# Attention and routed experts on one core: the second block's gathers in one run, and transposed probabilities in two tiles

## The chip, the core and the metric

The kernel runs on one core of one Trainium2 chip. The metric is the device time of one launch in microseconds, lower is better. Two executions of the same kernel differ by some tenths of a per cent.

## What is computed

Attention with rotary embedding over 8 batches, 8 heads, 576 tokens and 64 columns a head, then a mixture of 8 experts over the 4608 tokens, each token to the one expert with the highest logit:

```python
q_rot, k_rot = rotate(q), rotate(k)
scores = matmul(q_rot, k_rot.T) / sqrt(64)
attn = exp(scores - max(scores)); attn /= sum(attn) + 1e-9
x = matmul(attn, v)                      # as 4608 rows of 512
logits = x @ w_gate + modality_bias[modality_id]
e_idx = argmax(logits, axis=1); gate_w = softmax(logits)[e_idx]
for e in range(8):
    mask = e_idx == e
    h = maximum(x[mask] @ w1[e], 0.0)    # 512 -> 1024
    out[mask] = gate_w[mask, None] * (h @ w2[e])   # 1024 -> 512
```

Every matmul is in float32, most as three products of a high and a low part.

## The kernel before

**Attention.** The outer loop runs over 32 pairs of heads (`n`; four pairs are one batch). For each pair TensorE computes the scores in nine units (`scores`, tile `ps`), DVE takes the row minimum of the negated scores (`rowmin`, `mn`), ACT the exponential (`expo`, tile `P`). TensorE transposes the probabilities (`fill`), and ACT and DVE copy them out of PSUM (`evac`): into `PH` for the first 512 keys, 128 partitions x 8 x 576 queries, and into `PD` for the last 64 keys. `AV` multiplies them with V in two halves, queries 0 to 255 and 256 to 575. `outp`, `ev` and `xout` turn the result, scale it and write a batch of rows to the table `X` in device memory.

**Routing.** After each batch a chain of small steps (`route`) finds each token's expert and its place in the expert's list. `scatter` then writes token number and gate weight to the table `TAB`, in five indirect DMAs a batch, issued by GpSimd (POOL).

**Experts.** The tokens are worked in blocks of 256 (`s`). The first eight blocks are planned from the first five batches alone (`plan0`), so that they can begin before the routing of the last batches is done; a second plan covers the rest. A block's steps: `m_ix` loads its rows of `TAB` (tiles `ix`, `xi`); `m_gather` computes row numbers on POOL (`iy`) and issues eight indirect DMAs of 128 rows x 128 columns from `X` to `XG`, of which the first four are one half of the block and the last four the other; there are two `XG`, for even and odd blocks. `m_tr` transposes a half on DVE, `m_tre` copies it to the high part on ACT and subtracts on DVE for the low part (`HL<-XG`). `m_load1` and `m_load2` load weights to `ST1` and `ST2`, only where the expert changes; `m_hi` converts to the high part on ACT (`W1H`, `W2H`), `m_lo` subtracts on DVE (`W1L`, `W2L`). `m_l1` is the first layer (tile `psH`, 96 matmuls), `m_l1e` its relu, `m_l2` the second layer (`psY`, 48 matmuls), ACT's scaling by the gate (`sc`) and an indirect DMA of the output rows, on POOL.

**Order.** TensorE, ACT, DVE and POOL take their instructions in the order in which they are written, and this order comes from numbers: each step is a job with a key, a time within its pair of heads (`KEYS`, `EDGE`, `MOE`), and the jobs are sorted. A key above `end=25.0` in the last pair puts a job into the part behind the cut, where attention's PSUM is handed over and the steps follow in order of their keys; after them the block loop `chain` runs. SyncE's queue is written in this order up to the cut, and is ordered by the scheduler behind it. `AFTER` adds waits to single gathers, for instance for the latest first-layer matmul of block 0 that stands ahead (`'l1', 0`).

Of the kernel before, what the change touches and what calls it, by code (L numbers as in the profile page):

```python
# [8 lines left out]
F32 = mybir.dt.float32  # L9
# [9 lines left out]
P = 128  # L19
B, H, S, D = 8, 8, 576, 64  # L20
# [129 lines left out]
        "A_FB": 13.315, "B_FB": 14.059, "AVA": 14.280, "RE": 14.638, "A_F3": 14.844, "B_F3": 15.844, "OTA": 16.826, "AVB": 19.635,  # L150
# [3 lines left out]
    },  # L154
# [41 lines left out]
    setdma=(-353.070, -199.654, -64.082, -129.156),  # L196
    consts=(28.166, 28.282),
    plan=(-34.727, 16.183, -5.857, -25.884),
    ix=(-13.525, 17.418, 11.679, 11.775),
    w1=(-33.501, -27.735, 15.231, -22.655),  # L200
    w2=(-4.011, 1.762, 12.647, -8.483),
    hi=(-22.046, 1.027, 19.870, 16.903),
# [5 lines left out]
    l1=(17.301, 17.002, 22.720, 21.734),  # L208
    l1e=(22.809, 22.869, 24.662, 24.647),
    w1n=(20.502, 24.643, 23.254, 22.825),  # L210
    place=(10.490, 11.490),
    rows=(5.189, -7.595, 2.778, 1.170, -0.984, 8.071, 5.429, 11.766, 24.719, 23.818, 21.468, 24.323, 19.920, 20.117, 22.957, 17.444,
        18.250, 23.228, 17.169, 21.813, 22.941, 24.907, 21.508, 22.829),
    pl=(-114.356, -102.856, -99.906, -88.406, -85.506, -73.956, -51.417, -48.907, -45.303),
    end=25.0,
)
AFTER = {(0, 3): (30, 'av', 0), (0, 4): (30, 'av', 0), (0, 5): (30, 'av', 1), (0, 6): (30, 'av', 1), (0, 7): (30, 'out', 1), (1, 0): ('l1', 0), (1, 1): ('l1', 0), (1, 2): ('l1', 0), (1, 3): ('l1', 0), (1, 4): ('l1', 0), (1, 5): ('l1', 0), (1, 6): ('l1', 0), (1, 7): ('l1', 0)}
PIN = "PE,Activation,DVE,Pool"


# [1 line left out]
def tile_attention_moe(ctx: ExitStack, tc: tile.TileContext, qk, v, mod, wg, mb, w1, w2, rope, cf, ci, out):  # L222
# [43 lines left out]
    pp = ctx.enter_context(tc.tile_pool(name="pp", bufs=1))  # L266
# [7 lines left out]
    def place(i, name, **kw):  # L274
        return places[i].enter_context(tc.tile_pool(name=name, bufs=1, reuse_waits="tile", **(dict(side="right") if i == 0 else {}), **kw))
# [4 lines left out]
            [P, 8, DM], F32R, name="W2" + "HL"[i])  # L280

    P4 = pp.tile([P, S + 128], F32, name="P4")
    PD = pp.tile([P, S], F32, name="PD")
    Vs = [pp.tile([P, 2, 5, 64], F32, name=f"V{i}") for i in range(2)]


# [1 line left out]
    OT = [pp.tile([P, S], F32, name=f"oT{i}") for i in range(2)]  # L288
    pj = place(0, "pj")
    PJ = [pj.tile([P, 2 * S], F32, name=f"P{j}") for j in range(4)]  # L290
    PH = place(1, "ph").tile([P, 8, S], F32, name="PH")


    SL = [psS.tile([P, 2, 512], F32, name=f"ps{i}") for i in range(4)]
# [3 lines left out]
    def take(nm, bks):  # L298

        own = SLOTS[nm]  # L300
        if nm == "RK8":
            own, bks = own & 3, (own >> 2,)
        if not all((own, b) in idle for b in bks):
            if nm == "RK8":
                own, b = min(idle, key=idle.get)
                bks = (b,)
            else:
                own = min((i for i in range(4) if all((i, b) in idle for b in bks)), key=lambda i: max(idle[i, b] for b in bks))
        for b in bks:
            del idle[own, b]  # L310
        return (own, *bks) if nm == "RK8" else own

    def give(own, *bks):
        for b in bks:
            idle[own, b] = clock[0]
            clock[0] += 1
# [36 lines left out]
    def setup():  # L353
        g = nc.gpsimd
        v_ = nc.vector
        v_.memset(EPS, 1e-9)
        v_.memset(ZERO, 0.0)
        v_.memset(PD, 0.0)
        v_.memset(P4, 0.0)
        for t in Vs:  # L360
            v_.memset(t[64:128, 0, 4, :], 0.0)
            v_.memset(t[0:64, 1, 4, :], 0.0)
        v_.memset(G, 0.0)
        for t in HL + SW:
            for c in (0, TW - 64):
                v_.memset(t[:, :, c:c + 64].bitcast(F32), 0.0)
        for h in range(4):
            for s in range(2):
                g.tensor_copy(RW[s * 64:s * 64 + 64, h, :].rearrange("p (o c) -> p o c", o=2)[:, :, 0:32],
                              idf[s * 64:s * 64 + 64, s * 64:s * 64 + 64].rearrange("p (o c) -> p o c", o=2))  # L370
        g.memset(MI, 0)
        nonlocal TI
        TI = W1[0].rearrange("p a b -> p (a b)")[:, 0:(E + 1) * N * 2 // P].bitcast(I32)
        g.memset(TI, EMPTY)
        for t in XG:
            g.memset(t, 0.0)
        g.memset(ON, 1.0)
        g.memset(OH, 0.0)
        g.dma_start(out=CF, in_=cf)
        g.dma_start(out=VAL, in_=ci)  # L380
# [127 lines left out]
    def evac(n, f, g):  # L508
        d = st[n]
        ps = d[f][:, g]  # L510
        mine, other = (d.setdefault((f, x), []) for x in (g, 1 - g))
        give(d["at", f], g)


        def cp(o, i):
            mine.append((nc.vector.tensor_copy if g else acopy)(o, i).ins)  # L516
            for x in other:
                tc.declare_no_dep(mine[-1], x, reason="two banks")

        if f[1] in "0123":  # L520
            o = int(f[1]) * P + g * 64
            cp(PH[:, :, o:o + 64], ps.rearrange("p (a b) -> p a b", b=64))
            return
        tails = PD[:, 0:512].rearrange("p (j s c) -> p j s c", s=2, c=64)[:, :, g, :]
        if f == "FA":
            cp(tails[:, 0:2], ps[:, 0:128].rearrange("p (j c) -> p j c", c=64))
        else:
            cp(PH[:, 4 * g:4 * g + 4, 512:576], ps[:, 0:256].rearrange("p (k c) -> p k c", c=64))
            cp(PD[g * 64:g * 64 + 64, 512:576], ps[g * 64:g * 64 + 64, 256:320])
            cp(tails[:, 2:4], ps[:, 320:448].rearrange("p (j c) -> p j c", c=64))  # L530


    def AV(n, half):
        d = st[n]
        c0, c1 = (0, 256) if half == 0 else (256, 576)
        own = take("AV" + "AB"[half], (half,))
        pa = d["pa", half] = SL[own][:, half, :]
        d["at", "av", half] = own
        for kt in range(5):
            for hh in range(2):  # L540
                r = PH[:, 4 * hh + kt, c0:c1] if kt < 4 else PD[:, c0:c1]
                i = nc.tensor.matmul(pa[hh * 64:hh * 64 + 64, 0:c1 - c0], d["V"][:, hh, kt, :], r, start=(kt == 0), stop=(kt == 4))  # L542
                d.setdefault(("av", half), i.ins)

# [526 lines left out]

    K = KEYS
    setup()
    pinned = {getattr(mybir.EngineType, x) for x in PIN.split(",")}
    order = ExitStack()
# [14 lines left out]
    for n in range(NPAIR):  # L1090
# [7 lines left out]
        for f in ("F0", "F1", "F2", "F3", "FA", "FB"):  # L1098
            K_(f, fill, n, f)
            for g in range(2):  # L1100
                K_(f"{'AB'[g]}_{f}", evac, n, f, g)
        for w in range(2):
            c = "AB"[w]
            K_(f"AV{c}", AV, n, w)
            K_(f"OT{c}", avout, n, w)
            K_(f"EV{c}", ev, n, 1 - w)
# [12 lines left out]
        if n % 4 == 3:  # L1119
            K_("BIAS", bias, n // 4)  # L1120
            K_("XO", xout, n // 4)
            g = route(n // 4)
            steps = [(next, g, None)] * (NRK - (n == z))
            scats = [(scatter, n // 4, j) for j in range(5)]
            if n == z:

                g = plan()
# [7 lines left out]
    def Z(nm, i, f, *a):  # L1135
        J(MOE[nm][i], "moe", z, f, *a)
# [13 lines left out]
    g = plan0()  # L1150
    for i in range(9):
        Z("pl", i, next, g, None)
    for s in range(3):
        for i in range(8):
            Z("rows", 8 * s + i, m_gather, s, i // 4, i % 4, AFTER.get((s, i)))
    end = MOE["end"]
# [188 lines left out]
```

## Time and profile before

| | |
|---|---|
| Median of three runs | 922.65 us (919.7 to 923.22) |
| Profiled execution | 919.6 us |
| Its span on the core | 917.8 us |
| TensorE busy | 94% of the span |
| DVE, POOL, ACT busy | 75%, 71%, 69% |
| Mean granted TensorE clock | 0.983 |

Times in the rows are microseconds from the start of the span. PE is TensorE, PEld its weight loads, SPq the queue of DMA issues of SyncE. A row of a timeline has start, length, engine, line of the kernel, operation and tiles, and in brackets the idle time of the engine ahead of it with what ended that.

### The profile page before, as it was taken

The page shows a single profiled execution, that of the slowest core. Times are in us where ns is not written, and L with a number is a line of the kernel's source. Part 1 is how long each engine was busy: PE and PEld are TensorE (multiplying, and loading weights), DVE is VectorE, ACT ScalarE, POOL GpSimd, SP SyncE. Part 2 cuts the span into 40 slices and gives each one's busy share as a digit, 9 for nine tenths or more (in the row PEclk, how much of TensorE's full clock was granted, in tenths as well). Part 3 has the DMA queues.
Part 4 walks back from the last instruction along what each step waited for, and adds up shares of the span by engine and source line. Part 5 has one row for each costly group of instructions (what it writes and reads, how often), then busy time and mean ns, then how long its engine had stood idle before and what let it go on. Part 6 is the DMA issues. An engine that isn't in the chain of part 4 may idle for free.

```text
span 917.8 us, 25894 instructions
## 1 busy us (share of the span) xinstructions
PE 859.2 (94%) x9760; PEld 718.8 (78%) x9760; DVE 684.9 (75%) x1516; ACT 631.3 (69%) x1291; POOL 652.8 (71%) x494
## 2 busy tenths in 40 slices
PE   3899999999999999989994899999999999999995
PEld 2776777777777777766683799999999999999995
DVE  7777888888888889877781878766666666666662
ACT  2987988888988988978761555655555555555552
POOL 4989888998889899985466866766666666666400
PEclk9999999999999999999997799999999999999998
DMA  8776768978798887957612921127525112511240
GB/s 270 198 216 159 233 183 204 193 206 202 162 232 184 209 184 206 218 146 195 179 16 38 233 86 41 56 80 236 201 93 185 58 47 93 185 46 38 85 159 15
DMA packets 82466, 136.91 MB, mean 149 GB/s; under 512 B 28795, under 2 KB 53517, under 8 KB 81308
## 3 DMA queue, kind: packets, MB, share of 16 engines
q1 hardware_dynamic: 71740, 114.08, 47.2%
q0 software_dynamic: 9248, 19.46, 7.1%
q8 instruction: 79, 1.29, 0.6%
q10 hardware_dynamic: 1344, 1.62, 0.6%
q14 instruction: 55, 0.45, 0.2%
HBM read 138.16 MB, written 19.51 MB: 172 GB/s over the span
## 4 chain that ended last, share of the span: by engine, by line
PE 50%; issue 2%; POOL 1%; DVE 1%; DMA 1%; ACT 1%; POOLq 0%; DVEq 0%; ACTq 0%
PE psH L1020 22%; PE psY L1043 21%; PE ps L542 3%; PE ps L459 2%; PE ps L482 1%; POOL XG L956 1%; PE ps L1020 1%; DMA TAB<-VAL,oi 1%; PE ps L577 0%; DMA XG<-X,iy 0%; POOL TAB L694 0%; ACT PH L419 0%; DVE HL L416 0%; ACT P L477 0%; DVE X L589 0%
## 5 line engine op out<-in xcount | busy, mean ns | idle before, releaser
L477 ACT ACTIVATE P<-sc,mn 128x576 f32<-128x576 f32 x288 | 219.6, 766 | 5.9 <-DVE mn L468 4.8
L468 DVE CUSTOM_DVE_ANT_1 sc<-ps,ZERO 128x576 f32<-128x576 f32 x288 | 206.5, 748 | 21.8 <-PE ps L459 9.3
L1020 PE MATMUL psH<-HL,W1H 128*128 128x256 f32 x1152 | 205.2, 281 | 15.9 <-ACT W1H L419 15.9
L956 POOL DMA_INDIRECT XG<-X,iy x148 | 178.8, 1208 | 50.1 <-issue 36.7
L1020 PEld LDWEIGHTS psH<-HL,W1H 128*128 128x128 f32 x1152 | 178.9, 190 | 17.9 <-ACT W1H L419 16.4
L459 PE MATMUL ps<-SW 64*128 64x288 f32 x960 | 169.0, 311 | 14.7 <-DMA SW<-HL 12.5
L459 PE MATMUL ps<-HL 64*128 64x288 f32 x960 | 169.5, 311 | 5.8 <-DVE mn L468 2.1
L1020 PE MATMUL psH<-HL,W1L 128*128 128x256 f32 x576 | 162.1, 281 | 0.5 <-DVE W1L L416 0.5
L416 DVE TENSOR_TENSOR W1L<-ST,W1H 128x1024 fp32r<-128x1024 f32 x76 | 90.2, 1221 | 81.7 <-ACT W1H L419 81.6
L459 PEld LDWEIGHTS ps<-SW 64*128 64x128 f32 x960 | 135.5, 189 | 19.2 <-DMA SW<-HL 13.1
L459 PEld LDWEIGHTS ps<-HL 64*128 64x128 f32 x960 | 135.7, 189 | 11.3 <-issue 5.7
L542 PE MATMUL ps<-PH,V 128*64 128x320 f32 (+1 forms) x1024 | 138.2, 412 | 3.4 <-ACT P L477 2.1
L1048 POOL DMA_INDIRECT out_dram<-sc,ix x36 | 43.7, 1213 | 115.9 <-ACT sc L1046 100.0
L482 PEld LDWEIGHTS ps<-idf,P 64*128 64x128 f32 x2624 | 96.3, 139 | 33.3 <-ACT P L477 12.4
L1043 PE MATMUL psY<-W2L,SW 128*128 128x512 f32 (+1 forms) x304 | 118.0, 388 | 0.0
L1043 PE MATMUL psY<-W2H,SW 128*128 128x512 f32 (+1 forms) x304 | 116.7, 384 | 0.0
L482 PE MATMUL ps<-idf,P 64*128 64x64 f32 x2624 | 108.9, 226 | 7.5 <-ACT P L477 3.5
L516 DVE COPY PH<-ps 128x512 f32<-128x512 f32 (+1 forms) x160 | 98.4, 630 | 17.4 <-PE ps L482 12.2
L1020 PEld LDWEIGHTS psH<-HL,W1L 128*128 128x128 f32 x576 | 109.5, 190 | 0.8 <-DVE W1L L416 0.8
L436 POOL TENSOR_TENSOR HL<-ST,HL 128x1152 fp32r<-128x1152 f32 x31 | 82.4, 2657 | 38.9 <-ACT HL L419 38.8
L542 PEld LDWEIGHTS ps<-PH,V 128*64 128x64 f32 x1024 | 69.5, 136 | 50.3 <-issue 5.2
L419 ACT ACTIVATE PH<-ps 128x512 f32<-128x512 f32 (+1 forms) x160 | 85.5, 551 | 33.4 <-PE ps L482 25.4
(200 smaller groups left out, 1578.3 us busy)
## 6 DMA issues: line engine op xcount, KB each, us to landing
ST<-in_moe_w_dram SPq DMA_DIRECT2D x152, 512.0 KB
ST<-in_qk_dram SPq DMA_DIRECT2D x62, 576.0 KB
SW<-HL SPq DMA_DIRECT2D x124, 216.0 KB
V<-in_v_dram SPq DMA_DIRECT2D x32, 256.0 KB
X<-X SPq DMA_DIRECT2D x8, 1024.0 KB
XG<-X,iy POOLq DMA_INDIRECT x148, 3.1
V<-in_v_dram SPq DMA_DIRECT2D x64, 16.0 KB
X<-XT SPq DMA_DIRECT2D x16, 64.0 KB
```

The lines of the kernel that those rows point to most:

```text
L416: nc.vector.tensor_tensor(o, a, b, op=ALU.subtract)
L419: return nc.scalar.activation(o, i, AF.Copy, scale=scale)
L436: e.tensor_tensor(d["HL"][:, 1, o], a, d["HL"][:, 0, o].bitcast(F32), op=ALU.subtract)
L459: nc.tensor.matmul(ps[:, g, 0:288], t[:, wq, q0:q0 + P], t[:, wk, k0:k0 + 288], start=(m == 0), stop=(m == len(L) - 1))
L468: nc.vector.tensor_tensor_reduce(sc, d.pop(("S", u))[:, :, 0:288], ZERO.unsqueeze(2).to_broadcast([P, 2, 288]), 1.0, FMAX, ALU.add, ALU.mi ...
L477: nc.scalar.activation(p, sc.rearrange("p a b -> p (a b)"), AF.Exp, bias=mn, scale=-1.0, accum_out=d["sum"][:, u:u + 1])
L482: nc.tensor.transpose(ps[:, g, c:c + 64], src[r, k0:k0 + P], idf[r, r])
L516: mine.append((nc.vector.tensor_copy if g else acopy)(o, i).ins)
L542: i = nc.tensor.matmul(pa[hh * 64:hh * 64 + 64, 0:c1 - c0], d["V"][:, hh, kt, :], r, start=(kt == 0), stop=(kt == 4))
L956: inst = nc.gpsimd.indirect_dma_start(out=XG[s % 2][:, t, g, :], out_offset=None, in_=X.rearrange("n (i f) -> (n i) f", f=P)[0:rows], in_o ...
L1020: l1_[s] = nc.tensor.matmul(ps[:, i, :], w[:, c, f0:f0 + P], x[:, c, :], start=(m == 0), stop=(m == 11)).ins
L1043: nc.tensor.matmul(ps, hx[:, c, t * P:(t + 1) * P], x[:, c, h * w:h * w + w], start=(m == 0), stop=(m == 23))
```

## The change

It has two parts.

In the first the keys of the gathers of blocks 1 and 2 (`rows`, numbers 8 to 23) are set anew: block 1's eight stand in one run at 17.360 to 17.430, block 2's at 25.150 and up, behind the cut. The waits of block 1's gathers for block 0's matmuls (`AFTER`) go, the index load of block 1 (`ix`) moves a little ahead of the run, and the first scatter of the seventh batch (`SC0`) moves behind the cut.

In the second `PH` and `PD` become two tiles each, one for queries 0 to 255 and one for 256 to 575; `AV` reads the tile of its half.

```diff
-        "RK11": 71.745, "RK12": 78.963, "RK13": 82.481, "RK14": 82.519, "SC0": 82.645,
+        "RK11": 71.745, "RK12": 78.963, "RK13": 82.481, "RK14": 82.519, "SC0": 83.052,
...
-    ix=(-13.525, 17.418, 11.679, 11.775),
+    ix=(-13.525, 17.300, 11.679, 11.775),
...
-AFTER = {(0, 3): (30, 'av', 0), ..., (0, 7): (30, 'out', 1), (1, 0): ('l1', 0), ..., (1, 7): ('l1', 0)}
+AFTER = {(0, 3): (30, 'av', 0), ..., (0, 7): (30, 'out', 1)}
...
-    PD = pp.tile([P, S], F32, name="PD")
+    PD = [pp.tile([P, n], F32, name=f"PD{i}") for i, n in enumerate((256, 320))]
...
-    PH = place(1, "ph").tile([P, 8, S], F32, name="PH")
+    ph = place(1, "ph")
+    PH = [ph.tile([P, 8, n], F32, name=f"PH{i}") for i, n in enumerate((256, 320))]
...
-        v_.memset(PD, 0.0)
+        for t in PD:
+            v_.memset(t, 0.0)
...
-            o = int(f[1]) * P + g * 64
-            cp(PH[:, :, o:o + 64], ps.rearrange("p (a b) -> p a b", b=64))
+            h, o = divmod(int(f[1]), 2)
+            o = o * P + g * 64
+            cp(PH[h][:, :, o:o + 64], ps.rearrange("p (a b) -> p a b", b=64))
...
-                r = PH[:, 4 * hh + kt, c0:c1] if kt < 4 else PD[:, c0:c1]
+                r = PH[half][:, 4 * hh + kt, :] if kt < 4 else PD[half]
```

POOL, where attention ends and block 0 is at work, before (`XG_76` is the buffer of block 1, `XG_75` that of block 2; `TAB` rows are scatters):

```order
L694 DMA TAB<-VAL,oi 41472x2
L948 TENSOR_SCALAR iy<-xi,CF 128x8
L956 DMA XG_76<-X,iy 128x128
L956 DMA XG_75<-X,iy 128x128
L956 DMA XG_76<-X,iy 128x128 x2
L694 DMA TAB<-VAL,oi 41472x2
L956 DMA XG_76<-X,iy 128x128
L956 DMA XG_75<-X,iy 128x128 x2
L694 DMA TAB<-VAL,oi 41472x2
L956 DMA XG_75<-X,iy 128x128 x2
L956 DMA XG_76<-X,iy 128x128
```

These stood behind the row numbers and the first gather of block 2, and behind them came one more gather of block 2, the last three of block 1 and a last one of block 2. The same place on POOL now (the lines are three further on):

```order
L697 DMA TAB<-VAL,oi 41472x2 x2
L951 TENSOR_SCALAR iy<-xi,CF 128x8
L959 DMA XG_76<-X,iy 128x128 x8
L697 DMA TAB<-VAL,oi 41472x2 x3
L686 CAST oi<-of 128x5
L1051 DMA out_dram<-sc,ix 4608x512
L951 TENSOR_SCALAR iy<-xi,CF 128x8
L959 DMA XG_75<-X,iy 128x128 x8
L697 DMA TAB<-VAL,oi 41472x2 x5
```

Block 1's eight gathers follow two scatters and its row numbers; block 2's follow three more scatters and block 0's first output write.

SyncE's queue behind the cut, before (`ix` and `xi` are the index loads of the fifth block, `X` and `XT` the write of the last batch's rows, the last row the first weights of block 2):

```order
L930 ISA
L930 DMA ix<-TAB 128x4
L932 ISA
L932 DMA xi<-TAB 128x1x16
L601 DMA X<-XT 64x8x32
L599 DMA X<-X 128x2048
L601 DMA X<-XT 64x8x32
L972 ISA
L972 DMA ST_73<-in_moe_w_dram 128x4x256
```

And now:

```order
L602 DMA X<-X 128x2048
L604 DMA X<-XT 64x8x32 x2
L933 ISA
L933 DMA ix<-TAB 128x4
L935 ISA
L935 DMA xi<-TAB 128x1x16
L975 ISA
L975 DMA ST_73<-in_moe_w_dram 128x4x256
```

The row write moved ahead of the index loads, which now wait with it in the queue. On TensorE, ACT and DVE the order is the same as before, but for one more memset at the start.

More of the change, by code (lines that the diff above doesn't have):

```diff
@@ L211 @@
     place=(10.490, 11.490),
-    rows=(5.189, -7.595, 2.778, 1.170, -0.984, 8.071, 5.429, 11.766, 24.719, 23.818, 21.468, 24.323, 19.920, 20.117, 22.957, 17.444,
-        18.250, 23.228, 17.169, 21.813, 22.941, 24.907, 21.508, 22.829),
+    rows=(5.189, -7.595, 2.778, 1.170, -0.984, 8.071, 5.429, 11.766, 17.360, 17.370, 17.380, 17.390, 17.400, 17.410, 17.420, 17.430,
+        25.150, 25.160, 25.170, 25.180, 25.190, 25.200, 25.210, 25.220),
     pl=(-114.356, -102.856, -99.906, -88.406, -85.506, -73.956, -51.417, -48.907, -45.303),
@@ L216 @@
 )
-AFTER = {(0, 3): (30, 'av', 0), (0, 4): (30, 'av', 0), (0, 5): (30, 'av', 1), (0, 6): (30, 'av', 1), (0, 7): (30, 'out', 1), (1, 0): ('l1', 0), (1, 1): ('l1', 0), (1, 2): ('l1', 0), (1, 3): ('l1', 0), (1, 4): ('l1', 0), (1, 5): ('l1', 0), (1, 6): ('l1', 0), (1, 7): ('l1', 0)}
+AFTER = {(0, 3): (30, 'av', 0), (0, 4): (30, 'av', 0), (0, 5): (30, 'av', 1), (0, 6): (30, 'av', 1), (0, 7): (30, 'out', 1)}
 PIN = "PE,Activation,DVE,Pool"
@@ L520, in evac @@
         if f[1] in "0123":
-            o = int(f[1]) * P + g * 64
-            cp(PH[:, :, o:o + 64], ps.rearrange("p (a b) -> p a b", b=64))
+            h, o = divmod(int(f[1]), 2)
+            o = o * P + g * 64
+            cp(PH[h][:, :, o:o + 64], ps.rearrange("p (a b) -> p a b", b=64))
             return
-        tails = PD[:, 0:512].rearrange("p (j s c) -> p j s c", s=2, c=64)[:, :, g, :]
+        tails = PD[f == "FB"][:, 0:256].rearrange("p (j s c) -> p j s c", s=2, c=64)[:, :, g, :]
         if f == "FA":
-            cp(tails[:, 0:2], ps[:, 0:128].rearrange("p (j c) -> p j c", c=64))
+            cp(tails, ps[:, 0:128].rearrange("p (j c) -> p j c", c=64))
         else:
-            cp(PH[:, 4 * g:4 * g + 4, 512:576], ps[:, 0:256].rearrange("p (k c) -> p k c", c=64))
-            cp(PD[g * 64:g * 64 + 64, 512:576], ps[g * 64:g * 64 + 64, 256:320])
-            cp(tails[:, 2:4], ps[:, 320:448].rearrange("p (j c) -> p j c", c=64))
+            cp(PH[1][:, 4 * g:4 * g + 4, 256:320], ps[:, 0:256].rearrange("p (k c) -> p k c", c=64))
+            cp(PD[1][g * 64:g * 64 + 64, 256:320], ps[g * 64:g * 64 + 64, 256:320])
+            cp(tails, ps[:, 320:448].rearrange("p (j c) -> p j c", c=64))
     def AV(n, half):
```

## The prediction

> **What bounds the kernel now.** I read the busy shares first, then a table of stretches of 24 us, the list of waits, the chain of waits in order of time, and then, for the one stretch that stood out, each engine's instructions in order of time.
>
> ```profile
> PE 859.2 (94%) x9760; PEld 718.8 (78%) x9760; DVE 684.9 (75%) x1516; ACT 631.3 (69%) x1291; POOL 652.8 (71%) x494
> ...
> 480.00:504.00 24.00, 12.45 (x88) 9.81 (x86) 5.06 (x9) 3.48 (x5) 17.54 (x17) 0.81 0.30 39
> 504.00:528.00 24.00, 19.17 (x122) 18.01 (x123) 19.58 (x37) 13.51 (x20) 19.07 (x15) 0.77 0.94 227
> 528.00:552.00 24.00, 24.00 (x153) 21.59 (x152) 17.46 (x32) 13.04 (x16) 14.99 (x12) 1.00 0.27 80
> ```
>
> The columns of the stretches are the length, then busy time of PE, weight loads, DVE, ACT and POOL, the granted clock, the DMA share and GB/s. TensorE is the bound: 94% busy, and without a gap in the stretch from 528 us. The one large hole is between the first and the second expert block: 11.6 us lost in one stretch and 4.8 in the next, with the clock at 0.81 and 0.77. The list of waits names it:
>
> ```profile
> PE psH L1020 <- ACT W1H L419: 15.9, 1, 15.9
> ...
> PE ps L542 <- ACT PH L419: 0.7, 1, 0.7
> ```
>
> The columns are the sum, the times and the longest. One wait of 15.9 us, by name for the weight conversion W1H. The chain of waits shows what was late behind that name:
>
> ```profile
> 498.23 2.56 DMA XG<-X,iy
> ...
> 500.92 0.72 DVE XG L1001
> ...
> 501.71 1.12 ACT HL L419
> ...
> 502.86 2.08 DVE HL L416 x2
> ...
> 507.26 1.06 ACT W1H L419
> ...
> 534.74 11.20 PE psH L1020 x96
> ```
>
> The last gather of block 1 starts on POOL at 498.23 and lands at 500.79; 0.13 us later DVE transposes it, and everything up to W1H stands behind that in the in-order queues of DVE and ACT. TensorE had been done since 492.45:
>
> ```profile
> 492.06 0.39 PE L1043 MATMUL psY<-W2L,SW 128*128 128x512 f32 x1
> 508.37 0.80 PE L1020 MATMUL psH<-HL,W1H 128*128 128x256 f32 x2 [15.92 <-ACT W1H L419]
> ...
> 523.48 0.40 PE L1043 MATMUL psY<-W2H,SW 128*128 128x512 f32 x1
> ```
>
> **The change: the gathers.** The sum follows POOL. These rows tell what it did at the times that the new run takes:
>
> ```profile
> 467.92 1.35 POOL L948 TENSOR_SCALAR iy<-xi,CF 128x8 int32<-128x8 int32 x1
> 469.54 1.09 POOL L956 DMA_INDIRECT XG<-X,iy  x1 [0.28 <-POOL iy L948]
> 470.94 5.23 POOL L694 DMA_INDIRECT TAB<-VAL,oi  x1 [0.31 <-issue]
> ...
> 479.54 2.57 POOL L956 DMA_INDIRECT XG<-X,iy  x1 [0.30 <-issue]
> 482.41 1.01 POOL L956 DMA_INDIRECT XG<-X,iy  x1 [0.30 <-issue]
> ...
> 504.46 1.37 POOL L1048 DMA_INDIRECT out_dram<-sc,ix  x1 [2.38 <-ACT sc L1046]
> ```
>
> And beside them DVE:
>
> ```profile
> 470.60 1.21 DVE L416 TENSOR_TENSOR W1L<-ST,W1H 128x1024 fp32r<-128x1024 f32 x1
> ...
> 474.07 1.21 DVE L416 TENSOR_TENSOR W2L<-ST,W2H 128x1024 fp32r<-128x1024 f32 x1
> ...
> 478.88 2.34 DVE L416 TENSOR_TENSOR W2L<-ST,W2H 128x1024 fp32r<-128x1024 f32 x2
> ...
> 483.10 0.19 DVE L680 TENSOR_REDUCE of<-rk 128x5 f32<-128x40 f32 x1
> ```
>
> An indirect DMA takes POOL about 1.01 us, with 0.30 to the next. Two took 5.23 and 2.57: both began while DVE ran its 128x1024 weight splits, and both ended 0.9 us after the last of these (475.28 to 476.17, 481.22 to 482.11). I take it that a split holds them.
>
> DVE's order does not change, so I put the eight new gathers on POOL's old times. The index row stays at 467.92. Gather 1 is at 469.54. Gather 2 takes the place of the scatter at 470.94 and is held to 476.17. Gathers 3 and 4 start at about 476.5 and 477.8. Gather 5 starts at 479.1, is held as the one at 479.54 was, and ends at 482.1. Gathers 6, 7 and 8 start at 482.4, 483.7 and 485.05. With 2.56 us to landing the last is there at 487.6, against 500.79: 13.2 us earlier. The three scatters and seven gathers of block 2 that stood between come behind; the scatters write table rows of a later plan, for which nothing waits here.
>
> Gathers 1 to 4 are the block's first half, so its transpose can run right after 483.29, and only the second half waits. From the landing to the end of the splits HL<-XG (502.86 + 2.08 = 504.94) it was 4.15 us with both halves behind it; with one half done before it is 0.13 + 0.70 + 0.1 + 1.1 + 1.1 = about 3.1. From there to the first matmul nothing changes: 508.37 - 504.94 = 3.43. So block 1 starts at 487.6 + 3.1 + 3.4 = 494.1, **14.3 us earlier**, and TensorE's gap shrinks from 15.9 to about 1.65 us. What is late next is the same chain, with its last link still the gather.
>
> **The clock.** Block 1's first layer took 523.48 - 508.37 = 15.1 us, where the next block's 96 matmuls took 11.20. I put TensorE's windows beside that, cut where the granted clock changes:
>
> ```profile
> 23.71:27.12 3.41, 1.11 (x20) 0.99 0.97 272
> 27.12:30.54 3.42, 3.28 (x36) 0.51 0.90 268
> 443.48:446.89 3.41, 1.97 (x48) 1.00 0.67 193
> 491.27:494.68 3.41, 1.18 (x6) 1.00 0.37 32
> ...
> 508.33:511.75 3.42, 2.92 (x12) 0.50 1.38 132
> ```
>
> Here the columns are length, TensorE busy, clock, DMA share, GB/s. The changes of the clock lie on one grid of 3.41 us (27.12, 494.68 and 515.16 are 137 and 6 steps apart). After a stretch with 1.11 or 1.18 us busy it was halved; after 1.97 it stayed. After 3.28 busy it came back; after 2.92 it did not. So the old gap cost block 1 two stretches at half speed. Of the 3.9 us excess about 0.7 is the wait for W1L and six router matmuls; at full clock the W1L wait grows to 0.8 us, since the two matmuls ahead of it take half as long. The layer then takes 11.2 + 0.8 + 0.2 = 12.2 us, **2.9 us less**: 14.3 + 2.9 = 17.2.
>
> Whether the clock holds depends on where the grid falls, and I assume that the kernel does not set that. The new hole is 1.65 us, then 0.45 of matmuls, then 0.8 of waiting: a stretch that holds all of it has 1.0 us busy and would be followed by half clock, one that holds half would not. I make that even. The price is one stretch, since the next is full: 1.7 us. So the gain is 15.5 or 17.2; I take the middle, 16.3.
>
> The Trainium skill, page "TensorE: Matmul & The Clock Gate", section "Why this matters for your kernels", asks for no TensorE gaps over about 3 us and halves the clock after one idle window. By that rule a hole of 1.65 us costs nothing and the sum is 17.2. The trace disagrees on the size: at 27.12 and 494.68 the clock fell behind stretches with a third of their time busy.
>
> **The third block, block 2.** Its gathers now stand behind block 1's run, behind three scatters (three times 1.31 us, to about 490) and behind the first output write, which waits for ACT. In the trace that write started 3.54 us after the transposes (500.92 to 504.46); now it stands at about 490.5, so the run begins near 492.7.
>
> ```profile
> 514.09 2.05 POOL L956 DMA_INDIRECT XG<-X,iy  x1 [0.27 <-POOL iy L948]
> ...
> 526.18 1.38 POOL L956 DMA_INDIRECT XG<-X,iy  x1 [0.30 <-issue]
> ...
> 527.93 1.26 DVE L1001 STREAM_TRANSPOSE XG<-XG 128x512 f32<-128x512 f32 x2
> ```
>
> And of all gathers, from issue to landing:
>
> ```profile
> DMA to landing us min/median/max: 2.5/3.1/7.0
> ```
>
> A run of eight beside such splits took 13.5 us (514.09 to 527.56). So the last starts at about 504.8 and lands between 507.3 and 511.8. Block 2's first matmul stood at 534.74, now at 517.5, and needs the rows 4.0 us ahead, at 513.5. The cover is 1.7 to 6.2 us, where it was over 20; I cost it at nothing, and each us beyond costs one.
>
> **SyncE.** The last batch's X write moves ahead of the two index loads of the fifth block. It waits for DVE's X, which comes before the splits that free ST1.
>
> ```profile
> 507.45 0.64 SPq L601 DMA_DIRECT2D X<-XT  x1
> ...
> 509.61 5.12 SPq L972 DMA_DIRECT2D ST<-in_moe_w_dram  x4
> ```
>
> Two more issues of some 0.5 us each fit into the 1.5 us between these rows. Nothing, at most 0.5 us.
>
> **The split tiles.** They change no order on TensorE, ACT or DVE in the attention part, and by the order no wait. The most that separate tiles could win is the 0.7 us that AV waited for a PH copy (above); the most that they could lose is a rival. I take zero. The one new memset runs in the idle time before the first input:
>
> ```profile
> 5.65 0.66 DVE L428 TENSOR_TENSOR ST<-ST 128x480 f32<-128x480 f32 x1 [1.22 <-DMA ST<-in_qk_dram]
> ...
> L516 DVE COPY PH<-ps 128x512 f32<-128x512 f32 (+1 forms) x160 | 98.4, 630 | 17.4 <-PE ps L482 12.2
> ```
>
> **Sum.** The profiled execution took 919.6 us; less 16.3 is 903.3. It is at the fast end of the runs shown, 3 us below their median of 922.65; less 16.3 the median gives 906.4. I say 905.
>
> **Rivals.**
> A, the run isn't held. If the 5.23 us had another cause than the splits, the gathers go at 1.31 us each, the last starts at 478.7 and lands at 481.3, and TensorE goes from block 0 into block 1 without a gap, at 492.45, with W1L ready. The layer then ends at 503.9 instead of 523.48: 19.6 us, 900. For it: the short scatters beside other DVE work. Against it: two rows that end 0.9 us after a split. The Trainium skill gives a rule for this: "DMA: Bandwidth & Descriptors", section "SWDGE vs HWDGE vs iDMA", has VectorE lock GpSimd out while it runs in a 2-port mode, and "VectorE: DVE Perf Modes", section "Why `tensor_tensor` can't do 2×_2P or 4×", says that an operation on two tensors, as the split is, cannot run so. By these the run isn't held; the 5.23 us speaks against it. 12%.
> B, the run is held longer. Gather 4 starts at 477.8, 1.1 us ahead of the split at 478.88; if it is caught too, one more gather goes behind 482.1, and with 3.1 instead of 2.56 us to landing the last arrives 1.9 us later. The gap is 3.5 us, the clock falls for two stretches as before, and the gain is 14.3 - 1.9 = 12.4: 907 to 910. 18%.
> C, the third block is late. With every gather at 2.57 + 0.30 the run ends at 515.7 and lands by 519.8 at the slowest: 6.3 us of new wait and up to 2.5 at half clock, so a gain of 8.4: 911 to 914. It decides from a landing after 513.5. 7%.
> D, slower: the copies into the split PH. The strides of the rows that they write change from 576 to 256 and 320 words. A pair takes (480 - 24) / 32 = 14.25 us, DVE's copies L516 98.4 / 32 = 3.1 of it. In the stretch from 100 to 400 us (columns: length, DVE busy, clock, DMA share, GB/s)
>
> ```profile
> 100.00:400.00 300.00, 257.96 (x777) 1.00 0.81 194
> ```
>
> DVE idles 42 of 300 us, 2.0 of a pair. The copies would have to grow from 630 to about 1,170 ns, 2.66 us a pair, before DVE bounds each pair by 0.66 us more, 21 us in all, and the time is 927. No row shows such a copy. 3%.
> E, no change: TensorE waits as long for something else, say W1H's source. But all of that chain hangs on the transposes. 3%.
>
> **Chances.** The forecast has 57%: 15.5 to 17.2 us, from either base 902 to 907. With A and B the range is 900 to 910.5, and what is left out is C, D and E with 13%. Over 0.5% (4.6 us, about what a measurement can tell from no change) faster are the forecast, A, B and C: 94%; within it E, 3%; slower D, 3%.
>
> **What would show it.** Right: eight gathers on POOL from about 469.5 to 486 in the new trace, one of them near 5 us and one near 2.6; the wait of the psH matmuls for W1H under 3 us instead of 15.9; block 1's first layer 12 to 14 us; no hole in the stretch 504 to 552; the attention part of the same length up to 468.9. Wrong: a last landing after 490, a new wait ahead of block 2's first layer, or longer PH copies.

## The result, and the profile after

The changed kernel took 906.96 us, the median of four runs (906.03 to 910.65), against 922.13 of the kernel before beside it (919.7 to 923.22). The medians lie 15.2 us apart. The ratio, which is worked out from the single executions and not from the medians, is 0.9847, 95% interval 0.9812 to 0.9881, or 14.1 us; so are the ratios below, with the two slowest executions of e3_early left out. The forecast was 905.0 with 900.0 to 910.5. The profiled execution of the changed kernel took 906.03, its span is 904.2 us. Its line numbers are three further on than before, two in the small helpers.

TensorE's list of waits (sum, times, longest), where the 15.9 us stood:

```profile
PE psH L1023 <- DVE mx L635: 1.7, 1, 1.7
...
PE psH L1023 <- DVE W1L L418: 0.8, 1, 0.8
```

The long wait is 1.7 us now, and the wait for W1L behind it has grown to 0.8, both as forecast. The name DVE mx is no cause: the chain of waits (start, length, what) shows the same links as before, with the last gather's landing at their head.

```profile
486.30 2.57 DMA XG<-X,iy
488.89 0.72 DVE XG L1004
...
489.69 1.16 ACT HL L421
490.88 1.10 DVE HL L418
...
494.29 1.06 ACT W1H L421
495.37 1.24 DVE W1L L418
...
508.15 11.20 PE psY L1046 x48
519.35 11.20 PE psH L1023 x96
```

POOL's timeline shows the run of eight. Its row numbers, its first two gathers, its fifth and its last:

```profile
469.20 1.48 POOL L951 TENSOR_SCALAR iy<-xi,CF 128x8 int32<-128x8 int32 x1
470.96 1.10 POOL L959 DMA_INDIRECT XG<-X,iy  x1 [0.28 <-POOL iy L951]
472.37 5.16 POOL L959 DMA_INDIRECT XG<-X,iy  x1 [0.31 <-issue]
...
480.45 2.93 POOL L959 DMA_INDIRECT XG<-X,iy  x1 [0.30 <-issue]
...
486.30 1.01 POOL L959 DMA_INDIRECT XG<-X,iy  x1 [0.30 <-issue]
```

Gather 2 takes 5.16 us and gather 5 2.93, where the others take 1.00 to 1.10. DVE's last split ahead of the end of each:

```profile
475.42 1.21 DVE L418 TENSOR_TENSOR W2L<-ST,W2H 128x1024 fp32r<-128x1024 f32 x1
...
480.15 2.34 DVE L418 TENSOR_TENSOR W2L<-ST,W2H 128x1024 fp32r<-128x1024 f32 x2
```

The splits end at 476.63 and 482.49, the gathers 0.90 and 0.89 us later. And the stretches that had the hole (columns as in the prediction):

```profile
480.00:504.00 24.00, 21.57 (x167) 18.70 (x166) 18.49 (x35) 12.89 (x18) 19.51 (x18) 1.00 0.51 136
504.00:528.00 24.00, 24.00 (x160) 21.84 (x159) 17.66 (x25) 13.47 (x18) 19.37 (x17) 1.00 0.51 166
```

TensorE is busy 21.57 and 24.00 us where it was 12.45 and 19.17, at full clock.

The span shrank by 13.6 us, less than what the change gave at its place. A mark ahead of that place is the rank matmul of the seventh batch (`OH,UT`), a mark behind it the start of block 1's second layer. Between them lay 523.64 - 461.15 = 62.49 us before and 508.15 - 462.42 = 45.73 now: 16.8 us less. Two things went the other way in this pair of executions. The first mark itself came 1.27 us later. And each later second layer took 11.20 us instead of 11.10 (the row at 508.15 is the first), 17 of them, 1.7 us. 16.8 - 1.3 - 1.7 = 13.8. The two kernels run once more (e5 and e6 below) show that neither of the two belongs to the change.

### The profile page after: what moved, and what is told of

Same layout as the page of the kernel before. It is cut to its first block, busy times and chain, and to the rows that moved or that the text cites. A ratio compares the mean times of both kernels' runs of the same rounds, so it can differ in the third digit from the quotient of the medians.

```text
span 904.2 us, 25898 instructions
## 1 busy us (share of the span) xinstructions
PE 858.1 (95%) x9760; PEld 716.1 (79%) x9760; DVE 684.7 (76%) x1517; ACT 631.2 (70%) x1291; POOL 647.9 (72%) x494
## 4 chain that ended last, share of the span: by engine, by line
PE 49%; issue 2%; POOL 1%; DVE 1%; ACT 1%; DMA 0%; POOLq 0%; DVEq 0%; ACTq 0%
PE psH L1023 22%; PE psY L1046 22%; PE ps L545 2%; PE ps L461 2%; PE ps L484 1%; POOL XG L959 1%; DMA XG<-X,iy 0%; PE ps L580 0%; ACT PH L421 0%; ACT P L479 0%; DVE X L592 0%; POOL TAB L697 0%; POOL iy L951 0%; DVE W1L L418 0%; ACT HL L421 0%
## 5 line engine op out<-in xcount | busy, mean ns | idle before, releaser
L959 POOL DMA_INDIRECT XG<-X,iy x148 | 185.1, 1250 | 50.1 <-issue 36.3
L1023 PE MATMUL psH<-HL,W1H 128*128 128x256 f32 x1152 | 202.7, 279 | 1.7 <-DVE mx L635 1.7
L1023 PEld LDWEIGHTS psH<-HL,W1H 128*128 128x128 f32 x1152 | 176.7, 188 | 3.6 <-ACT W1H L421 2.1
L461 PEld LDWEIGHTS ps<-SW 64*128 64x128 f32 x960 | 135.8, 190 | 19.9 <-DMA SW<-HL 13.8
L1051 POOL DMA_INDIRECT out_dram<-sc,ix x36 | 48.8, 1354 | 105.4 <-ACT sc L1049 66.8
L1046 PE MATMUL psY<-W2L,SW 128*128 128x512 f32 (+1 forms) x304 | 119.9, 394 | 0.0
```

The lines of the kernel that those rows point to most:

```text
L461: nc.tensor.matmul(ps[:, g, 0:288], t[:, wq, q0:q0 + P], t[:, wk, k0:k0 + 288], start=(m == 0), stop=(m == len(L) - 1))
L959: inst = nc.gpsimd.indirect_dma_start(out=XG[s % 2][:, t, g, :], out_offset=None, in_=X.rearrange("n (i f) -> (n i) f", f=P)[0:rows], in_o ...
L1023: l1_[s] = nc.tensor.matmul(ps[:, i, :], w[:, c, f0:f0 + P], x[:, c, :], start=(m == 0), stop=(m == 11)).ins
L1046: nc.tensor.matmul(ps, hx[:, c, t * P:(t + 1) * P], x[:, c, h * w:h * w + w], start=(m == 0), stop=(m == 23))
```

## The experiments

They were made in three sets, each with its own runs of the kernel before; ratios are to those. The expectations count the batches from 0, so that their sixth batch is the seventh of the text, and what e12's calls the router matmul is the rank matmul.

| Run | Median us | Before us | Ratio, 95% interval |
|---|---|---|---|
| e1_gathers_only | 920.43 | 928.63 | 0.9902 (0.9866 to 0.9937) |
| e2_tiles_only | 930.14 | 928.63 | 1.001 (0.9988 to 1.0032) |
| e3_early | 929.78 | 928.63 | 0.9998 (0.9967 to 1.003) |
| e4_late | 923.94 | 928.63 | 0.9921 (0.9892 to 0.995) |
| e5_after_again | 908.33 | 924.56 | 0.9812 (0.9781 to 0.9843) |
| e6_before_again | 923.73, one run | 924.56 | |
| e7_early_again | 903.37 | 924.56 | 0.9762 (0.9731 to 0.9793) |
| e8_copies | 904.29 | 924.56 | 0.9762 (0.9723 to 0.9802) |
| e9_gathers_again | 909.0 | 923.1 | 0.9856 (0.9827 to 0.9884) |
| e10_waits_kept | 909.37 | 923.1 | 0.9851 (0.9823 to 0.9878) |
| e11_third_late | 911.02 | 923.1 | 0.9879 (0.9846 to 0.9912) |
| e12_late_again | 913.88 | 923.1 | 0.9897 (0.9864 to 0.9929) |

### One part of the change alone

```diff
 # e1 and e9, from before: SC0, ix, rows and AFTER as in the change; PH, PD one tile each
+    rows=(..., 17.360, ..., 17.430, 25.150, ..., 25.220),
 # e2, from before: PH and PD as in the change; SC0, ix, rows and AFTER as before
+    PH = [ph.tile([P, 8, n], F32, name=f"PH{i}") for i, n in enumerate((256, 320))]
```

> The kernel before with the first part of the change alone: new keys for the gathers, no waits on them, PH and PD as one tile each. Theory: the gather run is the whole gain, so 906 to 908 us (0.984 of before), with TensorE's wait ahead of block 1 at 1.7 us and W1L's at 0.8. Rival: the split tiles cost the 0.10 us by which each later second layer (psY, 48 matmuls) is longer in the changed kernel's profile (11.20 against 11.10, 17 of them, 1.7 us): then 905.2 here, and its profile shows 11.10. Second rival: the split tiles bring part of the gain, by shorter PH and PD waits: then 908.5 or more.

> The kernel before with the first part of the change alone, once more, since TensorE stuttered in e1_gathers_only. Theory: the gather run is the whole gain and the split tiles nothing: 0.981 to 0.985 of before, as the changed kernel in its two comparisons (0.9847, 0.9812). Rival: the split tiles carry a part: 0.989 or more, as e1_gathers_only read (0.9902).

> The kernel before with the second part alone: PH and PD in two tiles by queries, gathers and waits as before. Theory: no change, 921 to 923 us (0.998 to 1.002 of before), the 15.9 us wait stays. Rival: the tiles cost 0.10 us in each later second layer: 924 us, second layers of 11.20. Second rival: the tiles help AV's wait of 0.7 us: 921.4, which is hardly to be told from none.

The gathers alone gave 0.9902 in the first set and 0.9856 in the last; the whole change gave 0.9847 and 0.9812. The tiles alone gave 1.001. The time of e1 missed its forecast of 0.984, and that of e9 lies just above its 0.981 to 0.985. In the waits of e1 the mechanism is the changed kernel's to a tenth:

```profile
PE psH L1020 <- issue: 3.2, 5, 1.1
...
PE psH L1020 <- ACT W1H L419: 1.7, 1, 1.7
...
PE psH L1020 <- DVE W1L L416: 0.8, 1, 0.8
```

and e2 keeps the old one:

```profile
PE psH L1023 <- ACT W1H L421: 16.0, 1, 16.0
```

The first row of e1 is part of what spoiled its time. In the first set TensorE stuttered: a few matmuls, then a gap that ends in nothing that the profile shows. In e1 these lie between 558.9 and 564.5 us, far behind the change. From block 1's second layer to the end of the span e1 took 400.1 us, e9 393.3. e9, without them, ends the question within its interval: the first part is the gain. The tiles alone gain at most 0.1% by e2's interval (0.9988 to 1.0032). Together with the gathers the times don't bound them as closely (0.9856 against 0.9812 or 0.9847), but no row shows a gain: the copies PH took 630 ns before and after, and AV's wait of 0.7 us stayed.

The rival by which the tiles cost 0.10 us in each second layer had its sign in both profiles: these layers took 11.10 us in e1 and 11.20 in e2. It falls by e6 and e5, the two kernels once more, unaltered.

> The kernel before, unaltered, for a second profile of it. Theory: the 15.9 us wait ahead of block 1 as in the first profile, and the start of block 0's first layer within 6 us of 468.9. If the stutters by the reason 'issue' belong to the chip, they can show here too; if they come with the gather run, they do not. Second layers of 11.10 or of 11.20 us.

> The changed kernel once more, unaltered, beside the kernel before. Theory: the gain of the gather run holds on any chip, 0.983 to 0.991 of before; the second layers' 11.20 us belongs to the execution, and either 11.10 or 11.20 may show. Rival: the stutters of TensorE that the first four experiments show (gaps of 0.4 to 1.1 us by the reason 'issue', several in a row) come with the gather run: then they show here too, between 470 and 570 us, and not in the kernel before.

In the chain of e6, the kernel before, a second layer behind block 1 reads

```profile
549.28 11.20 PE psY L1043 x48
```

and in that of e5, the kernel after,

```profile
533.74 11.10 PE psY L1046 x48
```

So the 0.10 us of a second layer go with the execution, the other way round than in the first two profiles. The rank matmul was at 465.01 us in e6 and at 464.22 in e5, where the first profiles had 461.15 and 462.42: that mark moves by 4 us between executions of one kernel. No stutter by 'issue' stands in the expert part of e5 to e12. So the gather run doesn't bring the stutter by itself, as e5's rival had it. But in the first set all three kernels with the run had it (e1, e3 and e4), and e2 with the old gathers did not; that the two are linked there isn't excluded.

### The run earlier, and later

```diff
 # e3 and e7, from after
-    plan=(-34.727, 16.183, ...   ix=(-13.525, 17.300, ...   w1=(-33.501, -27.735, 15.231,
+    plan=(-34.727, 12.700, ...   ix=(-13.525, 12.710, ...   w1=(-33.501, -27.735, 12.660,
-    rows=(..., 17.360, 17.370, ..., 17.430,
+    rows=(..., 12.750, 12.755, ..., 12.785,
 # e4 and e12, from after
+    rows=(..., 22.010, 22.020, ..., 22.080,
```

> The changed kernel with block 1's row numbers and eight gathers moved ahead of the rank step and the five scatters of the sixth batch on POOL, to about 461.4 us; order of the other engines unchanged. Theory: gap and W1L wait come from the last gather's landing alone. Gathers 1 to 4 go at 1.31 us each from 461.8, those that start while HL<-XG or W1L splits run on DVE (467.2 to 470.5, 472.0 to 476.6) are held to 0.9 us behind them, and the last lands by 480.4 at the latest. DVE transposes at 484.5 in its order, W1H and W1L are ready by 492, and block 1 follows block 0 with no gap: 1.67 + 0.76 = 2.4 us less than the changed kernel, 904.5 us. Rival: block 1 waits for something else that the landing hid (W1H's source, ACT's order): less than 0.5 us gained, 906.5 to 907.

> Block 1's gathers ahead of the rank step and the scatters, as in e3_early, beside the changed kernel on the same chip. If the loss in e3_early (time as before, TensorE stuttering from 469 to 480 us) was chance, this is 2.4 us faster than e5_after_again. If the early gathers, which run beside the last attention matmuls, cause the stutters, it is again 5 to 10 us slower than e5_after_again, with the gaps by the reason 'issue' at the same place.

e3 was as slow as before, and the stutter hit it hardest. TensorE's timeline at the end of attention:

```profile
471.25 0.51 PE L580 MATMUL ps<-RW,oT 64*64 64x72 f32 x4 [0.44 <-issue]
472.70 0.52 PE L580 MATMUL ps<-RW,oT 64*64 64x72 f32 x5 [0.93 <-issue]
474.16 0.35 PE L580 MATMUL ps<-RW,oT 64*64 64x72 f32 x1 [0.94 <-issue]
```

One to five matmuls every 1.45 us, and the clock was at half for 20.5 us from 465.8 on. The same kernel in the next set has none of this, and is 5.0 us faster than the changed kernel beside it (903.37 against 908.33), where 2.4 was expected. So the stutter isn't a steady property of the early run; whether that run makes it worse where it occurs stays open. POOL and the chain of e7:

```profile
462.69 1.06 POOL L959 DMA_INDIRECT XG<-X,iy  x1 [0.28 <-POOL iy L951]
...
467.97 1.97 POOL L959 DMA_INDIRECT XG<-X,iy  x1 [0.30 <-issue]
470.24 1.89 POOL L959 DMA_INDIRECT XG<-X,iy  x1 [0.30 <-issue]
472.44 1.00 POOL L959 DMA_INDIRECT XG<-X,iy  x1 [0.30 <-issue]
473.74 4.48 POOL L959 DMA_INDIRECT XG<-X,iy  x1 [0.30 <-issue]
```

```profile
483.18 11.35 PE psY L1046 x48
494.53 5.60 PE psH L1023 x48
```

The last gather ends at 478.2, and block 1's first layer follows block 0's second without a gap. From mark to mark it is 506.00 - 463.18 = 42.82 us, 2.9 less than in the changed kernel's first profile and 4.4 less than in e5, which had a stretch at half clock; the 2.4 were the two waits alone, without the clock. This is the version that beats both kernels.

> The changed kernel with block 1's run behind all five scatters of the sixth batch instead of two. Theory: by the rule for held indirect DMAs scatter 3 (469.4) is held to 471.4, scatter 5 to 477.5 and gather 3 to 483.4; gather 8 starts at 488.9 and lands at 491.5, 2.6 us later than in the changed kernel; TensorE's gap grows from 1.67 to 4.3 us, and the granted clock falls to half for one or two stretches of 3.41 us: 906.96 + 2.6 + 1.7 to 3.4 = 911 to 913 us. Rival one, the clock doesn't fall for a gap of 4.3 us: 909.6. Rival two, indirect DMAs are not held by DVE but run into another limit (the weight loads of SyncE at 470.6 to 476): then all five scatters and eight gathers shift by 3 times 1.31 = 3.9 us, the landing is at 492.8 and the time 912.6 to 914.

> Block 1's run behind all five scatters once more, since e4_late shared its chip with stutters and its first wait was shortened by a half clock ahead of it. Theory: last gather 2.6 us later than in the changed kernel (23.9 us behind the router matmul of the sixth batch there, 26.5 here), a gap of 4.3 us and half clock for one to three stretches of 3.41 us behind it: 4.3 to 7.7 us slower than the changed kernel, 0.986 to 0.991 of before. Rival, the clock does not fall for such a gap: 2.6 us slower.

TensorE's timeline in e12:

```profile
502.18 0.69 PE L1023 MATMUL psH<-HL,W1H 128*128 128x256 f32 x2 [4.44 <-ACT W1H L421]
```

The hole, TensorE's wait ahead of block 1, is 4.44 us where 4.3 was expected, the last gather starts 492.95 - 466.44 = 26.5 us behind the rank matmul, as expected, and from mark to mark it is 51.07 us, 5.3 more than in the changed kernel. In e4 the last gather stood at 26.6, but half clock ahead of it kept TensorE in block 0 for longer, and the hole was 2.91. Its ratio, 0.9921, lies above the 0.988 to 0.990 that 911 to 913 us are of the 922.13 they were worked out beside; with stutters at 535 to 539 and 562 to 565 us that says nothing of the rivals. In e12 and e10 (below) 2.6 and 1.3 us of later start are 2.8 and 1.25 of hole, so a microsecond later is about a microsecond of hole, and beyond that the clock decides.

### The waits, and the third block

```diff
 # e10, from after: AFTER as before
+AFTER = {(0, 3): ..., (1, 0): ('l1', 0), ..., (1, 7): ('l1', 0)}
 # e11, from after
-        25.150, 25.160, ..., 25.220),
+        85.150, 85.160, ..., 85.220),
```

> The changed kernel with the waits of block 1's gathers for block 0's matmuls kept. Theory: the wait is for the second of four parts of block 0's first layer, 5.6 us after its start at 470.2 (clock of the changed kernel's profile), while the second gather was held till 477.5 anyway; so gather 1 starts at 475.8 and is held to 477.5, the last starts at 487.6 instead of 486.3 and lands at 490.2, the gap is 3.0 instead of 1.7 us: 1.3 us slower than the changed kernel, up to 3 with a stretch at half clock; 0.983 to 0.986 of before. So the order on POOL is the gain, and the waits that went are nearly nothing. Rival: the waits were what set the old time: 8 us or more slower than the changed kernel.

POOL and TensorE in e10:

```profile
481.10 1.10 POOL L959 DMA_INDIRECT XG<-X,iy  x1 [6.13 <-issue]
...
491.89 1.01 POOL L959 DMA_INDIRECT XG<-X,iy  x1 [0.30 <-issue]
```

```profile
500.92 0.50 PE L1023 MATMUL psH<-HL,W1H 128*128 128x256 f32 x2 [2.92 <-ACT W1H L421]
```

The first gather waits 6.13 us, and the hole is only 1.25 us larger than in the changed kernel (2.92 against 1.67), because a gather was held at that time anyway. The order on POOL is nearly all of the gain, not the waits that went. No run takes the waits away and leaves the old order.

> The changed kernel with block 2's gathers behind the five scatters of the last batch too, 6.5 us later on POOL. In the changed kernel's profile block 2's last gather starts at 505.3 and ends at 506.7, lands at about 509.3, DVE's transposes come at 512.44 in their order, the splits HL<-XG end at 516.5 and block 2's first layer starts at 519.35. Theory: a landing up to 515.3 costs nothing, so the cover was 6.0 us; here the last starts at 512 and lands at 515.9: 0.6 us of new wait ahead of block 2's first layer, at most 3; 0.982 to 0.987 of before. Rival: the cover was at the low end of the forecast, 1.7 us: 4.8 us of wait, and half clock behind it, 7 us slower than the changed kernel.

The chain of e11, at block 2's last gather:

```profile
513.38 6.05 DMA XG<-X,iy
...
519.51 0.72 DVE XG L1004
520.25 1.13 ACT HL L421
521.40 1.12 DVE HL L418
```

It started 1.4 us later than expected and took 6.05 us to land where 3.9 was assumed: at 519.43. TensorE waited 1.94 us for the high part and 0.75 for the low, and a stretch at half clock followed. The wait for the high part was three times my expected 0.6, and both together, 2.7, within the 3 given as the most; the ratio, 0.9879, lies just above the 0.982 to 0.987 expected. It says when the rows are needed: for the first matmul 519.43 - 1.94 = 517.5, about 2.0 us ahead of where it would have stood, and for neither part to be waited for 0.75 earlier, 2.7 ahead. In the changed kernel the transposes ran at 512.44 without a wait, so the cover there was at least 519.35 - 2.7 - 512.44 = 4.2 us. While this gather was landing the DMA engines were full (share 1.04 from 513.38 to 519.43); that this is why it took 6.05 us isn't shown.

### What holds an indirect DMA

```diff
 # e8, from after: block 0's eight low parts (W1L, W2L before the second block)
-            sub(W1[1][:, :, sl], ST1[:, :, sl], W1[0][:, :, sl].bitcast(F32))
+            nc.vector.tensor_copy(W1[1][:, :, sl], ST1[:, :, sl])
...
-            sub(W2[1][:, sl, :], ST2[:, sl, :], W2[0][:, sl, :].bitcast(F32))
+            nc.vector.tensor_copy(W2[1][:, sl, :], ST2[:, sl, :])
```

> The changed kernel with block 0's eight low parts of the weights (W1L, W2L before the second block) made by a DVE copy of the weights, one operand, where a subtraction of two stood; the subtraction is left out. Theory: what holds an indirect DMA on POOL is a DVE operation on two operands in SBUF: then only gathers that start while HL<-XG runs are held, gather 8 starts at about 479 and lands at 481.5 (on the clock of the changed kernel's profile), the 1.67 us gap and the 0.76 us W1L wait go, and the time is 2.4 us below e5_after_again. Rival, by the rule that copies within SBUF are what shuts POOL out: gathers are held to the end of the copies as before, some 5 us in all, with no gain beyond the shorter copies' own 2 us. Second rival: neither holds, it was the weight loads of SyncE (470.6 to 476): one gather still takes about 5 us.

POOL and DVE in e8:

```profile
476.67 2.25 POOL L959 DMA_INDIRECT XG<-X,iy  x1 [0.31 <-issue]
...
484.46 1.97 POOL L959 DMA_INDIRECT XG<-X,iy  x1 [0.30 <-issue]
486.73 1.00 POOL L959 DMA_INDIRECT XG<-X,iy  x1 [0.30 <-issue]
```

```profile
476.25 0.68 DVE L1001 CAST W1L<-ST 128x1024 fp32r<-128x1024 f32 x1
...
478.12 0.68 DVE L1004 CAST W2L<-ST 128x1024 fp32r<-128x1024 f32 x1
...
485.03 1.28 DVE L1004 CAST W2L<-ST 128x1024 fp32r<-128x1024 f32 x2
```

My theory, that only operations on two operands in SBUF hold a gather, fell: the copies hold it too, one from 476.67 to 478.92 and one to 486.43. Both end 0.12 us after the last copy (478.80, 486.31). So does the second rival: the four weight loads stand at the same place in SyncE's queue, and the long gather shrank from 5.16 to 2.25 us with the DVE work; the one at 484.46 was held when SyncE issued nothing (its next load came at 486.33). In e7 the gather at 472.44 took 1.00 us in the midst of those four loads (471.29 to 476.70). It is DVE's subtractions and copies between tiles in SBUF that hold POOL. The run was still short enough for no hole: 42.76 us from mark to mark, as in e7. The time itself says little, since DVE has less work here.

## Why the prediction was right

The marks and holes of the first two profiles and of those of the later sets together (us; e11, which is the changed kernel up to block 1, is left out; the last column counts stretches of 3.41 us at half clock between the marks):

| Run | Rank matmul to second layer of block 1 | Hole | Half clock |
|---|---|---|---|
| before | 62.49 | 15.92 | 6 |
| e6_before_again | 61.87 | 15.93 | 5 |
| after | 45.73 | 1.67 | 0 |
| e5_after_again | 47.22 | 1.61 | 1 |
| e9_gathers_again | 47.47 | 1.85 | 1 |
| e10_waits_kept | 48.53 | 2.92 | 1 |
| e12_late_again | 51.07 | 4.44 | 2 |
| e7_early_again | 42.82 | 0 | 0 |
| e8_copies | 42.76 | 0 | 0 |

**The gathers.** The step held nearly to the tenth. Taken back by the 1.27 us by which this execution was later, the last gather started at 485.03 (forecast 485.05) and landed at 487.6 (487.6), gather 5 was free at 482.11 (482.1), and block 1 began at 494.12 (494.1). That a DVE split holds the gather, and that one caught by a row of splits comes free 0.9 us behind the last, was right for both gathers of this run; e8 shows that the cause is wider than the split, and the last section that not every row holds to its end.

**The first layer.** Forecast at 12.2 us with the whole clock, it took 508.15 - 495.39 = 12.8, against 15.3 before (12.6 and 15.1 by the timeline's rows, from which the forecast came). The 2.9 us of this term were 2.5, mis-sized by 0.4. The rows put it into the first half of the layer: 2 and 46 matmuls took 0.50 and 5.63 us, where e7 did the 48 in 5.60.

**The clock.** The even chance was the right way to put it: after a hole of 1.6 to 1.9 us the clock stayed in the first profile, and in e1 and e11, and fell in e5 and e9. The price was 1.5 us (47.22 against 45.73) where 1.7 was forecast. So 16.8 us or 14.6 to 15.3 came off between the marks, for 17.2 or 15.5.

**The third block.** Costed at nothing, and it cost nothing. The working was too careful: the rows are needed 2.0 to 2.7 us ahead of the first matmul, not 4.0, since half of the block is split by then (e11).

**The split tiles and SyncE.** Nothing, as forecast (e2; no wait for SyncE's X write in TensorE's list).

**The sum.** Forecast 905 for 906.96. Of the 2.0 us 0.8 is the base: 905 and the gain of 16.3 make 921.3, between a profiled execution at the fast end and the median, and the median came out at 922.13. The other 1.1 is the gain, 15.2 us by the medians. From 922.13 the two cases give 904.9 and 906.6. How near a single comparison comes to 905 is in part luck: by the ratios the gain was 14.1 us in this one and 17.4 in e5's.

**The rivals.** A, the run not held, did not come true: two gathers were held. What it priced, no hole, is seen in e7, where the run is held too but goes earlier: the gain between the marks is 62.49 - 42.82 = 19.7 us, for the 19.6 worked out. B, held longer, is e10 by another way: 1.25 us more of hole. C came only where e11 made it. D and E showed in no row.

## What to carry to other kernels

When several transfers stand interleaved in one queue, ask which of them the next stage waits for, and put those in one run ahead of all that nothing waits for; here the order alone was worth 14 us (62.49 against e10's 48.53), and the waits that were removed with it 1 to 3, the clock included. Before placing a run of indirect DMAs, lay it beside DVE's rows: one that starts within subtractions or copies from SBUF to SBUF comes free only behind them, as a rule at the end of the row, so the last gather's time is found by counting which ones are caught. And move such a run until the hole is gone, not until it is small: the last 1.7 us of it cost 2.9 us, and 4.4 where the clock fell.

## What the runs showed of the hardware

**The clock goes by stretches of 3.41 us, and by how much of one is busy.** On the grid of each run's own clock changes, the stretch with most of the hole (length, TensorE busy, ..., clock), and in e5 and e12 what followed; first after, then e1, e5, e9, e10 and e12:

```profile
491.73:495.14 3.41, 1.99 (x9) 1.30 (x7) 2.71 (x9) 1.31 (x3) 2.65 (x4) 1.00 0.64 178
495.14:498.55 3.41, 2.40 (x18) 2.19 (x19) 3.30 (x8) 3.41 (x6) 2.73 (x3) 1.00 0.82 151
```

```profile
499.63:503.04 3.41, 1.74 (x9) 1.09 (x7) 2.67 (x10) 1.65 (x4) 2.63 (x4) 1.00 0.69 204
```

```profile
495.42:498.83 3.41, 1.03 (x6) 0.74 (x6) 2.73 (x7) 3.26 (x6) 2.68 (x3) 1.00 1.37 271
498.83:502.24 3.41, 3.41 (x18) 3.41 (x17) 3.41 (x5) 2.74 (x4) 2.80 (x3) 0.50 0.72 217
```

```profile
498.11:501.52 3.41, 1.14 (x7) 0.94 (x8) 2.85 (x7) 3.37 (x6) 2.80 (x3) 1.00 1.18 256
```

```profile
498.83:502.24 3.41, 0.56 (x3) 0.36 (x3) 2.79 (x7) 2.89 (x5) 2.53 (x4) 1.00 1.21 259
```

```profile
498.91:502.32 3.41, 0.14 (x1) 0.14 (x2) 2.70 (x9) 1.71 (x4) 2.74 (x4) 1.00 0.56 231
502.32:505.74 3.42, 2.85 (x12) 2.56 (x13) 3.35 (x7) 3.42 (x6) 2.81 (x3) 0.50 0.94 250
505.74:509.15 3.41, 3.41 (x17) 3.41 (x17) 3.21 (x6) 1.49 (x3) 2.80 (x3) 0.50 0.89 266
```

In these rows the clock stayed behind 1.74 us busy or more and halved behind 1.18 (from the prediction's rows) or less. At half clock 2.85 us busy did not bring it back. The border between is not sharp: behind 1.56 us the clock stayed in e6 (87.6 to 91.0), behind 1.67 it fell in e10 (280.4 to 283.8), and in e3's stutter it fell behind 2.09 (568.2 to 571.6). And in the first 18 us of a span none of this shows: in the changed kernel's first profile TensorE is busy for 1.15 us from 10.45 to 13.86, and the clock column stays at 1.00. The same hole of 1.6 us costs nothing or 1.5 us by where the grid falls.

The Trainium skill, page "TensorE: Matmul & The Clock Gate", section "What's actually happening", has a free-running window of 3413 ns, which these rows bear out, and the half clock after one idle window, which they do not: a window a third busy (e9, 1.14 us) was enough.

**DVE's subtractions and copies from SBUF to SBUF both hold POOL's gathers.** Behind splits a gather ended 0.9 us after the last, behind copies 0.12 us after. Not every row of splits holds to its end. The gather of e7 at 467.97 came free at 469.94, while two splits ran from 467.92 to 470.19. The one of the changed kernel at 497.84 came free at 499.23, 0.88 us behind the split that ended at 498.35, though the next began at 498.37. When a gather is caught by the next split too stays open. More than DMAs is held: POOL's row numbers `iy`, 0.27 us in e5 at 495.00, took 3.99 in e4 (481.10 to 485.09), to 0.14 us behind the last of four splits. Copies out of PSUM and transposes of XG held none: the gathers of e7 between 462.69 and 467.67 took 1.00 to 1.06 us beside them.

The Trainium skill, page "SBUF — State Buffer", section "🔬 SBUF: two separate sides", names both kinds, DVE operations in a 2-port mode and those with two SBUF inputs, the second only against a GpSimd operation that reads SBUF. Its part "A bandwidth-pool intuition that's wrong (but worth ruling out)" has a locked-out DMA end about 115 ns after a DVE copy. e8's 0.12 us agree with that; for the subtraction it gives no such number, and the rows show 0.9.

**The stutter.** In e1, e3 and e4 TensorE went for 3 to 11 us at a few matmuls per 0.73 or 1.45 us, for no releaser in the profile; in e2, in e5 to e12 and in the first two profiles nothing of it stands in the expert part. Its cause is open.
